# Keys in three chunks of 128 and one shared chunk of 64, instead of four chunks of 112, in an attention + MLP kernel

## The chip, the cores and the metric

The kernel runs on one core of a Trainium2 chip. The metric is the device time of one execution in microseconds (us). Timed runs of different kernels alternate with runs of the kernel before on the same chip.

## The reference

```python
# q, k, v: (8, 12, 448, 64) f32; w_in (768, 2048), w_out (2048, 768)
scores = (q @ k.transpose(0, 1, 3, 2)) / 8
attn = softmax(scores, axis=-1)
x = (attn @ v).transpose(0, 2, 1, 3).reshape(3584, 768)
h = x @ w_in
out = np.maximum(0.01 * h, h) @ w_out
```

## The kernel before

The unit of attention is a **pair** of heads (48 pairs, six to each of 8 batches). The MLP runs in eight **blocks** of 384 and 512 rows in turn; while block i runs on TensorE, the attention of batch i+1 is laid between its groups of matmuls in small bursts ("clusters").

```python
# load: three DMAs a pair, all on SP's queue; 448 rows = 112 partitions x 4 rows (1 KB runs)
for a, name, eng in zip((q, k, v), ("fq", "fk", "fv"), queues):
    t = ld_pool.tile([SC, 2, NSC, D], F32, name=name)
    eng.dma_start(out=..., in_=a[b, 2 * hp:2 * hp + 2].rearrange("h (p so) d -> p h (so d)", so=NSC))
# ... cut ...
def turn(dst, src):           # q and k of a pair by one transposing DMA (from pair 12 on)
    nc.sync.dma_start_transpose(out=dst.rearrange("p (c s) -> p c s", s=SC), in_=src)
# ... cut ...
def scores(u, c):             # one chunk of 112 keys, two heads side by side (64 rows each)
    ps = ps_s.tile([P, 2, 512], F32, name="sc")          # 3 buffers of 2 PSUM banks
    for j in range(2):
        nc.tensor.matmul(ps[:, j, :S], t[j*D:(j+1)*D, S+c*SC:S+c*SC+P], t[j*D:(j+1)*D, :S], ...)
def pv(u, j):                 # one head: 4 query chunks x 4 key chunks, 65 columns each
    ps = ps_g.tile([P, NSC, D + 1], F32, name="pv", tag="g")  # 2 banks, shared with the MLP
    for qc in range(NSC):
        for c in range(NSC):
            nc.tensor.matmul(ps[:, qc, :], e[:, at:at + P], vt[:, j, c, :], ...)
```

One cluster holds three score groups and one or two `pv`; four clusters serve three pairs. SP's queue issues, in program order, the loads, the transposes of q/k and of the attention's output x (the MLP reads x transposed, `xT`), and the stores.

The softmax here doesn't subtract the row's maximum and nothing guards it: scores larger than these inputs give would overflow.

## Time and profile before

| | before |
|---|---|
| time, median of the first 3 runs | 427.14 us (422.94 to 427.53) |
| span of the profiled run | 423.4 us |
| TensorE (PE) busy | 410.8 us (97%) |
| ScalarE (ACT) busy | 228.6 us (54%) |
| DMA issues a pair on SP | 3 loads, 2 transposes, and the stores |

The page's lines, and the chain of work in order of time, are shown in the prediction. A timeline line reads: start, duration, engine, line of the kernel, operation, output<-input, count. A name with q at the end ("SPq") is the engine's issuing of DMAs.

The table below is the yardstick: the time at which each MLP block's first matmul runs, from TensorE's timeline, as the length of each stretch. A wait in a block's first group counts in that block.

| us | start | block 0 (384) | 1 (512) | 2 (384) | 3 (512) | 4 (384) | 5 (512) | 6 (384) |
|---|---|---|---|---|---|---|---|---|
| before | 35.6 | 51.4 | 53.9 | 43.6 | 53.9 | 43.6 | 53.9 | 40.8 |

### The profile page before, as it was taken

The page shows a single profiled execution, that of the slowest core. Times are in us where ns is not written, and L with a number is a line of the kernel's source. Part 1 is how long each engine was busy: PE and PEld are TensorE (multiplying, and loading weights), DVE is VectorE, ACT ScalarE, POOL GpSimd, SP SyncE. Part 2 cuts the span into 40 slices and gives each one's busy share as a digit, 9 for nine tenths or more (in the row PEclk, how much of TensorE's full clock was granted, in tenths as well). Part 3 has the DMA queues.
Part 4 walks back from the last instruction along what each step waited for, and adds up shares of the span by engine and source line. Part 5 has one row for each costly group of instructions (what it writes and reads, how often), then busy time and mean ns, then how long its engine had stood idle before and what let it go on. Part 6 is the DMA issues. An engine that isn't in the chain of part 4 may idle for free.

```text
span 423.4 us, 9000 instructions
## 1 busy us (share of the span) xinstructions
PE 410.8 (97%) x3731; PEld 236.2 (56%) x3731; DVE 99.7 (24%) x271; ACT 228.6 (54%) x322; POOL 91.2 (22%) x168
## 2 busy tenths in 40 slices
PE   8889999999999999999999999999999999999995
PEld 3555656554556656554565656655465666654562
DVE  1542323320132212221132212321032211320021
ACT  4875772766724684467634486457652577214200
POOL 5493330530311211131131213131120200000000
PEclk9987999999999999999999999999999999999999
DMA  8999999995465947667365775768266420230022
GB/s 217 261 250 245 249 250 210 232 242 116 106 160 155 209 110 183 186 160 173 97 150 150 200 143 133 192 158 211 64 154 162 118 56 16 58 86 2 0 76 74
DMA packets 98506, 63.66 MB, mean 150 GB/s; under 512 B 55457, under 2 KB 94881, under 8 KB 98465
## 3 DMA queue, kind: packets, MB, share of 16 engines
q1 hardware_dynamic: 90928, 56.56, 54.7%
q0 software_dynamic: 7296, 6.29, 9.2%
q8 instruction: 29, 0.48, 0.5%
q10 hardware_dynamic: 240, 0.23, 0.2%
q14 instruction: 13, 0.10, 0.1%
HBM read 45.61 MB, written 11.01 MB: 134 GB/s over the span
## 4 chain that ended last, share of the span: by engine, by line
PE 92%; DMA 4%; DVE 1%; ACT 1%; SPq 0%; issue 0%; POOL 0%; ACTq 0%
PE mm L268 35%; PE mm L250 34%; PE pv L199 12%; PE sc L181 10%; DMA fk<-in_k_dram 3%; DMA fv<-in_v_dram 1%; PE tr L169 1%; DVE o L272 1%; DVE x L207 1%; ACT e L190 0%; SPq L97 0%; DVE rec L206 0%; PE tr L220 0%; DVE qkT L172 0%; POOL qkb L109 0%
## 5 line engine op out<-in xcount | busy, mean ns | idle before, releaser
L190 ACT ACTIVATE e<-sc 112x896 bf16<-112x896 f32 x192 | 164.7, 918 | 105.7 <-PE sc L181 105.4
L250 PE MATMUL mm<-xT,w_in_sb 128*128 128x384 bf16 (+1 forms) x768 | 150.6, 353 | 0.7 <-DVE x L207 0.7
L268 PE MATMUL mm<-w_out_sb,h 128*128 128x384 bf16 x896 | 150.5, 326 | 0.6 <-DVE x L207 0.3
L268 PEld LDWEIGHTS <-h 128*128 128x128 bf16 x896 | 85.8, 98 | 55.4 <-DVE x L207 0.5
L250 PEld LDWEIGHTS <-w_in_sb 128*128 128x128 bf16 x768 | 73.1, 98 | 66.6 <-DVE x L207 1.0
L254 ACT ACTIVATE h<-mm 128x384 bf16<-128x384 f32 (+1 forms) x128 | 69.7, 545 | 60.5 <-PE mm L250 60.5
L110 POOL CAST v<-fv 112x512 bf16<-112x512 f32 x48 | 29.6, 617 | 212.8 <-PE pv L199 187.3
L199 PEld LDWEIGHTS <-e 112*128 112x128 bf16 x1536 | 57.7, 99 | 30.1 <-issue 17.8
L199 PE MATMUL pv<-v,e 112*128 112x65 bf16 x1536 | 67.0, 196 | 2.6 <-ACT e L190 1.4
L272 DVE COPY o<-mm 128x384 f32<-128x384 f32 x56 | 31.2, 558 | 133.7 <-PE mm L268 133.7
L206 DVE RECIPROCAL rec<-pv 112x4 f32<-112x4 f32 x96 | 17.6, 183 | 159.2 <-PE pv L199 159.1
L181 PE MATMUL sc<-qkT 64*128 64x448 bf16 x384 | 50.2, 361 | 0.8 <-DVE qkT L172 0.4
L207 DVE TENSOR_TENSOR x<-pv,rec 112x256 bf16<-112x256 f32 x96 | 40.7, 424 | 3.3
L108 POOL CAST qkb<-fq 112x512 bf16<-112x512 f32 x47 | 28.9, 616 | 20.8 <-DMA qkT<-qkb 11.7
L109 POOL CAST qkb<-fk 112x512 bf16<-112x512 f32 x47 | 28.9, 616 | 11.3 <-DMA fk<-in_k_dram 11.2
L181 PEld LDWEIGHTS <-qkT 64*128 64x128 bf16 x384 | 13.7, 95 | 19.9 <-issue 10.4
L172 DVE COPY qkT<-tr 128x896 bf16<-128x896 bf16 x12 | 7.4, 620 | 11.7 <-PE tr L169 11.6
L169 PE MATMUL tr<-ident,qkb 112*128 112x112 bf16 x96 | 8.3, 236 | 1.4 <-POOL qkb L109 1.4
L169 PEld LDWEIGHTS <-qkb 112*128 112x128 bf16 x96 | 6.3, 110 | 3.8 <-POOL qkb L109 1.6
L135 PE MATMUL mm<-warm 128*128 128x512 bf16 x15 | 5.8, 531 | 1.2 <-DVE warm L130 1.2
L221 DVE COPY xT<-tr 128x448 bf16<-128x448 bf16 x9 | 3.5, 389 | 7.3 <-PE tr L220 7.3
L220 PE MATMUL tr<-ident,x 112*128 112x112 bf16 x36 | 3.7, 232 | 0.2
(17 smaller groups left out, 15.2 us busy)
## 6 DMA issues: line engine op xcount, KB each, us to landing
fq<-in_q_dram SPq DMA_DIRECT2D x48, 224.0 KB, 3.6
fv<-in_v_dram SPq DMA_DIRECT2D x48, 224.0 KB, 4.3
fk<-in_k_dram SPq DMA_DIRECT2D x47, 224.0 KB, 3.8
w_in_sb<-in_moe_w_in_dram POOLq DMA_DIRECT2D x4, 768.0 KB, 15.0
w_out_sb<-in_moe_w_out_dram POOLq DMA_DIRECT2D x4, 768.0 KB, 35.2
out_dram<-o SPq DMA_DIRECT2D x8, 336.0 KB, 3.0
out_dram<-o SPq DMA_DIRECT2D x8, 288.0 KB, 2.6
out_dram<-o SPq DMA_DIRECT2D x8, 240.0 KB, 3.2
```

The source lines that it names most:

```text
L108: by[0](qk_sb[u][:, 0].rearrange("p so h d -> p h so d"), fq)
L109: by[1](qk_sb[u][:, 1].rearrange("p so h d -> p h so d"), fk)
L110: by[2](v_sb[u % NV][:, :, :, :D], fv)
L169: nc.tensor.transpose(tr[:, i, ts(so, SC)], qk_sb[u][:, i, so], ident[:SC, :SC])
L181: nc.tensor.matmul(ps[:, j, :S], t[j * D:(j + 1) * D, S + c * SC:S + c * SC + P], t[j * D:(j + 1) * D, :S], start=True, stop=True,)
L190: nc.scalar.activation(e[:, :, c, :], sc_t.pop((u, c))[:SC, :, :S], AX.Exp, scale=scale)
L199: nc.tensor.matmul(ps[:, qc, :], e[:, at:at + P], vt[:, j, c, :], start=(c == 0), stop=(c == NSC - 1),)
L207: nc.vector.tensor_mul(x_t[u][:, :, j, :], ps[:SC, :, :D], rec.to_broadcast([SC, NSC, D]))
L250: nc.tensor.matmul(ps[:, :n], w_in_sb[:, kk, ts(m, P)], xT[:, kk, at:at + n], start=(kk == 0), stop=(kk == KD - 1),)
L254: nc.scalar.activation(h[:, m, :n], ps[:, :n], AX.Prelu, alpha=0.01)
L268: nc.tensor.matmul(ps[:, :NW], h[:, m, ts(c, P)], w_out_sb[:, m, ts(w, NW)], start=(m == 0), stop=(m == MD - 1),)
L272: nc.vector.tensor_copy(o[c][:, ts(w, NW)], ps[:, :NW])
```

## The change

Each head's 448 keys become three chunks of 128 and a rest of 64. The rests of both heads of a pair share one chunk: their k stand block-diagonally (128 rows of contraction), so one full-array matmul gives both heads' scores, and their v stand block-diagonally, so one product of 130 columns adds to both heads. A pair then has 3 full score groups and one half one instead of 4, 28 products instead of 32, and 3.5 exponentials' worth of columns instead of 4. The bursts become "events", two to a pair: event 0 has the first half of the last pair's products and three score groups; event 1 has the single score group and the second half.

```diff
-        for a, name, eng in zip((q, k, v), ("fq", "fk", "fv"), queues):
+        (the load of q, as before: cut)
+        for a, name, eng in ((k, "fk", queues[1]), (v, "fv", queues[2])):
+            t = ld_pool.tile([P, (2 * NKC + 1) * D], F32, name=name)
             eng.dma_start(
+                out=t[:, :2 * NKC * D].rearrange("p (h e) -> p h e", h=2),
+                in_=a[b, heads, :NKC * P].rearrange("h (p c) d -> p h (c d)", c=NKC),
             )
+            for h in range(2):
+                eng.dma_start(
+                    out=t[h * KR:(h + 1) * KR, 2 * NKC * D:], in_=a[b, 2 * hp + h, NKC * P:]
+                )
 ... (casts and zero fills cut)
-            turn(qkT[u % NQ][:, :QL], qk_sb[u].rearrange("p i so h d -> p (i so h d)"))
+            turn(qkT[u % NQ][:, :S], qk_sb[u % NC][:SC, :QC], SC)
+            turn(qkT[u % NQ][:, S:], qk_sb[u % NC][:, QC:], P)
 ...
+        if c == NKC:
+            nc.tensor.matmul(ps[:, 0, :S], t[:, keys], t[:, :S], start=True, stop=True)
+            return
 ...
+            nc.tensor.matmul(
+                ps[:, i].rearrange("p j d -> p (j d)"), e[:, at:at + P], vt[:, VL:],
+                start=True, stop=False,
+            )
 ... (first(), event() in place of cluster(): cut)
```

More of the change, by code (lines that the diff above doesn't have):

```diff
@@ L37 @@
     NW = DM // 2
+    NKC = 3
+    KR = S - NKC * P
     NU = B * HP
@@ L47 @@
     ld_pool = ctx.enter_context(tc.tile_pool(name="ld", bufs=5))
-    cast_pool = ctx.enter_context(tc.tile_pool(name="cast", bufs=4))
+    cast_pool = ctx.enter_context(tc.tile_pool(name="cast", bufs=1))
     v_pool = ctx.enter_context(tc.tile_pool(name="vones", bufs=1))
@@ L60 @@
     ps_g = ctx.enter_context(tc.tile_pool(name="ps_g", bufs=2, space=PSUM))
+    DV = D + 1
+    VL = 2 * NKC * DV
     NV = 5
-    v_sb = [v_pool.tile([SC, 2, NSC, D + 1], BF16, name=f"v{i}") for i in range(NV)]
+    v_sb = [v_pool.tile([P, VL + 2 * DV], BF16, name=f"v{i}") for i in range(NV)]
+    v_whole = [t[:, :VL].rearrange("p (h c d) -> p h c d", h=2, c=NKC) for t in v_sb]
     NE = 3
-    EL = 2 * NSC * S
-    e_sb = [exp_pool.tile([SC, EL + P - SC], BF16, name=f"e{i}") for i in range(NE)]
+    EW = 2 * NKC * S
+    EL = EW + S
+    e_sb = [exp_pool.tile([P, EL + P - SC], BF16, name=f"e{i}") for i in range(NE)]
+    NC = 4
+    QC = NSC * P
+    qk_sb = [cast_pool.tile([P, QC + (NKC + 1) * P], BF16, name=f"qkb{i}") for i in range(NC)]
     NQ = 4
-    QL = 2 * S
-    qkT = [qk_pool.tile([P, QL + P - SC], BF16, name=f"qkT{i}") for i in range(NQ)]
+    QL = S + (NKC + 1) * P
+    qkT = [qk_pool.tile([P, QL], BF16, name=f"qkT{i}") for i in range(NQ)]
     NX = 4 * S
@@ L85 @@
     raw = {}
-    qk_sb = {}
     def load(u, queues=(nc.sync,) * 3):
@@ L93, in load, with cast @@
         b, hp = divmod(u, HP)
-        raw[u] = []
-        for a, name, eng in zip((q, k, v), ("fq", "fk", "fv"), queues):
-            t = ld_pool.tile([SC, 2, NSC, D], F32, name=name)
+        heads = slice(2 * hp, 2 * hp + 2)
+        fq = ld_pool.tile([SC, 2, NSC, D], F32, name="fq")
+        queues[0].dma_start(
+            out=fq.rearrange("p h so d -> p h (so d)"),
+            in_=q[b, heads].rearrange("h (p so) d -> p h (so d)", so=NSC),
+        )
+        raw[u] = [fq]
+        for a, name, eng in ((k, "fk", queues[1]), (v, "fv", queues[2])):
+            t = ld_pool.tile([P, (2 * NKC + 1) * D], F32, name=name)
             eng.dma_start(
-                out=t.rearrange("p h so d -> p h (so d)"),
-                in_=a[b, 2 * hp:2 * hp + 2].rearrange("h (p so) d -> p h (so d)", so=NSC),
-            )
+                out=t[:, :2 * NKC * D].rearrange("p (h e) -> p h e", h=2),
+                in_=a[b, heads, :NKC * P].rearrange("h (p c) d -> p h (c d)", c=NKC),
+            )
+            for h in range(2):
+                eng.dma_start(
+                    out=t[h * KR:(h + 1) * KR, 2 * NKC * D:], in_=a[b, 2 * hp + h, NKC * P:]
+                )
             raw[u].append(t)
-    def cast(u, by=(nc.gpsimd.tensor_copy,) * 3):
+    def cast(u, by=(nc.gpsimd.tensor_copy,) * 2):
         if u >= NU:
@@ L106, in cast @@
         fq, fk, fv = raw.pop(u)
-        qk_sb[u] = cast_pool.tile([SC, 2, NSC, 2, D], BF16, name="qkb")
-        by[0](qk_sb[u][:, 0].rearrange("p so h d -> p h so d"), fq)
-        by[1](qk_sb[u][:, 1].rearrange("p so h d -> p h so d"), fk)
-        by[2](v_sb[u % NV][:, :, :, :D], fv)
+        t, vt = qk_sb[u % NC], v_sb[u % NV]
+        by[0](t[:SC, :QC].rearrange("p (so h d) -> p h so d", so=NSC, h=2), fq)
+        by[1](
+            t[:, QC:QC + NKC * P].rearrange("p (c h d) -> p h c d", c=NKC, h=2),
+            fk[:, :2 * NKC * D].rearrange("p (h c d) -> p h c d", h=2, c=NKC),
+        )
+        for h in range(2):
+            at, c0 = slice(h * KR, (h + 1) * KR), QC + NKC * P + h * D
+            by[1](t[at, c0:c0 + D], fk[at, 2 * NKC * D:])
+        nc.gpsimd.tensor_copy(
+            v_whole[u % NV][:, :, :, :D],
+            fv[:, :2 * NKC * D].rearrange("p (h c d) -> p h c d", h=2, c=NKC),
+        )
+        for h in range(2):
+            at, c0 = slice(h * KR, (h + 1) * KR), VL + h * DV
+            nc.gpsimd.tensor_copy(vt[at, c0:c0 + D], fv[at, 2 * NKC * D:])
     w_steps = []
@@ L139 @@
     make_identity(nc, ident)
-    for t in v_sb:
-        nc.gpsimd.memset(t[:, :, :, D:], 1.0)
+    for t in qk_sb:
+        nc.gpsimd.memset(t[:, QC + NKC * P:], 0.0)
+    for t, tw in zip(v_sb, v_whole):
+        nc.gpsimd.memset(tw[:, :, :, D:], 1.0)
+        nc.gpsimd.memset(t[:, VL:], 0.0)
+        for h in range(2):
+            nc.gpsimd.memset(t[h * KR:(h + 1) * KR, VL + h * DV + D:VL + (h + 1) * DV], 1.0)
     for t in e_sb:
         nc.gpsimd.memset(t[:, EL:], 0.0)
-    for t in qkT:
-        nc.gpsimd.memset(t[:, QL:], 0.0)
-    cast(0, (nc.vector.tensor_copy, nc.scalar.copy, nc.gpsimd.tensor_copy))
+    cast(0, (nc.vector.tensor_copy, nc.scalar.copy))
     load_w()
@@ L154, with turn @@
     NPE = 12
-    def turn(dst, src):
-        nc.sync.dma_start_transpose(out=dst.rearrange("p (c s) -> p c s", s=SC), in_=src)
+    def turn(dst, src, rows):
+        nc.sync.dma_start_transpose(out=dst.rearrange("p (c s) -> p c s", s=rows), in_=src)
     def dma_transposes(u):
         if NPE <= u < NU:
-            turn(qkT[u % NQ][:, :QL], qk_sb[u].rearrange("p i so h d -> p (i so h d)"))
+            turn(qkT[u % NQ][:, :S], qk_sb[u % NC][:SC, :QC], SC)
+            turn(qkT[u % NQ][:, S:], qk_sb[u % NC][:, QC:], P)
     def transposes(u):
@@ L165, in transposes @@
             return
-        tr = ps_g.tile([P, 2, S], BF16, name="tr", tag="g")
-        for i in range(2):
-            for so in range(NSC):
-                nc.tensor.transpose(
-                    tr[:, i, ts(so, SC)], qk_sb[u][:, i, so], ident[:SC, :SC]
-                )
-        nc.vector.tensor_copy(qkT[u % NQ][:, :QL], tr.rearrange("p i s -> p (i s)"))
+        tr = ps_g.tile([P, QL], BF16, name="tr", tag="g")
+        t = qk_sb[u % NC]
+        for so in range(NSC):
+            nc.tensor.transpose(tr[:, ts(so, SC)], t[:SC, ts(so, P)], ident[:SC, :SC])
+        for c in range(NKC + 1):
+            nc.tensor.transpose(
+                tr[:, S + c * P:S + (c + 1) * P], t[:, QC + c * P:QC + (c + 1) * P], ident
+            )
+        nc.vector.tensor_copy(qkT[u % NQ], tr)
     sc_t = {}
@@ L179, in scores, with expo @@
         sc_t[u, c] = ps
+        keys = slice(S + c * P, S + (c + 1) * P)
+        if c == NKC:
+            nc.tensor.matmul(ps[:, 0, :S], t[:, keys], t[:, :S], start=True, stop=True)
+            return
         for j in range(2):
+            at = slice(j * D, (j + 1) * D)
+            nc.tensor.matmul(ps[:, j, :S], t[at, keys], t[at, :S], start=True, stop=True)
+    def expo(u, c):
+        ps = sc_t.pop((u, c))
+        if c == NKC:
+            o, i = e_sb[u % NE][:, EW:EL], ps[:, 0, :S]
+        else:
+            e = e_sb[u % NE][:, :EW].rearrange("p (j c s) -> p j c s", j=2, c=NKC)
+            o, i = e[:, :, c, :], ps[:, :, :S]
+        nc.scalar.activation(o, i, AX.Exp, scale=scale)
@@ L181, in scores, with pv @@
+    def pv(u, half):
+        e, vt = e_sb[u % NE], v_sb[u % NV]
+        two = NSC // 2
+        ps = ps_g.tile([P, two, 2, DV], F32, name="pv", tag="g")
+        for i in range(two):
+            qc = half * two + i
+            at = EW + qc * SC
             nc.tensor.matmul(
-                ps[:, j, :S],
-                t[j * D:(j + 1) * D, S + c * SC:S + c * SC + P],
-                t[j * D:(j + 1) * D, :S],
-                start=True, stop=True,
-            )
-    def expo(u, c):
-        e = e_sb[u % NE][:, :EL].rearrange("p (j c s) -> p j c s", j=2, c=NSC)
-        nc.scalar.activation(e[:, :, c, :], sc_t.pop((u, c))[:SC, :, :S], AX.Exp, scale=scale)
@@ L192, in pv @@
-    def pv(u, j):
-        e, vt = e_sb[u % NE], v_sb[u % NV]
-        ps = ps_g.tile([P, NSC, D + 1], F32, name="pv", tag="g")
-        for qc in range(NSC):
-            for c in range(NSC):
-                at = (j * NSC + c) * S + qc * SC
-                nc.tensor.matmul(
-                    ps[:, qc, :], e[:, at:at + P], vt[:, j, c, :],
-                    start=(c == 0), stop=(c == NSC - 1),
-                )
-        if j == 0:
+                ps[:, i].rearrange("p j d -> p (j d)"), e[:, at:at + P], vt[:, VL:],
@@ L204, in pv @@
+                start=True, stop=False,
+            )
+            for j in range(2):
+                for c in range(NKC):
+                    at = (j * NKC + c) * S + qc * SC
+                    nc.tensor.matmul(
+                        ps[:, i, j, :], e[:, at:at + P], v_whole[u % NV][:, j, c, :],
+                        start=False, stop=(j == 1 and c == NKC - 1),
+                    )
+        if half == 0:
             x_t[u] = x_pool.tile([SC, NSC, 2, D], BF16, name="x")
-        rec = r_pool.tile([SC, NSC, 1], F32, name="rec")
@@ L206, in pv @@
-        nc.vector.reciprocal(rec, ps[:SC, :, D:])
+        rec = r_pool.tile([SC, two, 2, 1], F32, name="rec")
+        nc.vector.reciprocal(rec, ps[:SC, :, :, D:])
         nc.vector.tensor_mul(
-            x_t[u][:, :, j, :], ps[:SC, :, :D], rec.to_broadcast([SC, NSC, D])
+            x_t[u][:, ts(half, two)], ps[:SC, :, :, :D], rec.to_broadcast([SC, two, 2, D])
         )
@@ L215, in x_transposes @@
         if u >= NPE - 3:
-            turn(dst, x_t.pop(u).rearrange("p so h d -> p (so h d)"))
+            turn(dst, x_t.pop(u).rearrange("p so h d -> p (so h d)"), SC)
             return
@@ L291, in first @@
         load_w({2: 1, 3: 2, 4: 2, 5: 2}.get(u, 0))
+        scores(u, 2)
+        expo(u, 2)
         if u + 1 < HP:
             transposes(u + 1)
-        scores(u, 2)
         scores(u, 3)
-        expo(u, 2)
         expo(u, 3)
@@ L300, in first, with event @@
             pv(u - 1, 1)
-    def cluster(g):
-        t, r = divmod(g, 4)
-        u = 3 * t
-        chunks = [divmod(4 * u + 3 * r + x, NSC) for x in range(3)]
-        chunks = [(a, c) for a, c in chunks if a < NU]
-        heads = [[(u - 1, 0)], [(u - 1, 1)], [(u, 0), (u, 1)], [(u + 1, 0), (u + 1, 1)]][r]
-        heads = [(a, j) for a, j in heads if HP <= a < NU]
-        turned = {0: u - 2, 2: u - 1, 3: u}.get(r)
-        if turned is not None and HP <= turned < NPE - 3:
-            x_transposes(turned)
-        if len(heads) > 1:
-            pv(*heads.pop(0))
-        for a, c in chunks:
-            scores(a, c)
-        for a, c in chunks[:2]:
-            expo(a, c)
-        late.extend(chunks[2:])
-        for a, j in heads:
-            pv(a, j)
-            if j == 1 and a >= NPE - 3:
-                x_transposes(a)
-        if r < 3:
-            cast(u + 3 + r)
-            load(u + 5 + r)
-        transposes({3: u + 3, 0: u + 1, 1: u + 2}.get(r, NU))
-        if r > 0:
-            dma_transposes(u + 2 + r)
+    def event(g):
+        u, r = divmod(g, 2)
+        back = HP < u <= NU
+        if r == 0:
+            if HP < u - 1 < NPE - 3 + 1:
+                x_transposes(u - 2)
+            if back:
+                pv(u - 1, 0)
+            if u < NU:
+                for c in range(NKC):
+                    scores(u, c)
+                expo(u, 0)
+                expo(u, 1)
+                late.append((u, 2))
+            cast(u + 3)
+            load(u + 5)
+        else:
+            if u < NU:
+                scores(u, NKC)
+                expo(u, NKC)
+            if back:
+                pv(u - 1, 1)
+                if u - 1 >= NPE - 3:
+                    x_transposes(u - 1)
+            transposes(u + 1)
+            dma_transposes(u + 2)
     transposes(0)
@@ L340 @@
     x_transposes(u)
-    begin = [8 * (i + 1) + 3 for i in range(B)]
-    begin[0] = 8
+    begin = [2 * HP * (i + 1) + 3 for i in range(B)]
+    begin[0] = 2 * HP
     for i in range(B):
@@ L355, in catch_up @@
                 settle()
-                cluster(work[done])
+                event(work[done])
                 done += 1
```

## The prediction

> **What bounds the kernel now.** I read the page's busy table and slices first, then the groups, then the chain in order of time, and last the timelines of SP and of the first 40 us.
>
> ```profile
> PE 410.8 (97%) x3731; PEld 236.2 (56%) x3731; DVE 99.7 (24%) x271; ACT 228.6 (54%) x322; POOL 91.2 (22%) x168
> ...
> PE   8889999999999999999999999999999999999995
> ...
> DMA  8999999995465947667365775768266420230022
> ...
> PE 92%; DMA 4%; DVE 1%; ACT 1%; SPq 0%; issue 0%; POOL 0%; ACTq 0%
> ```
>
> The reader sees one full row: TensorE (PE). Nothing else is near its limit after slice 9 (some 95 us); before that the DMA row is full as well, and all of the chain's 4% of DMA lies there (two loads at 2.67 to 8.15 and 8.15 to 18.78 us). So from about 85 to 377 us only TensorE's own work counts; the first 35 us hang on loads, on the exponentials and on small waits.
>
> The chain in order of time, for the second MLP block (512 rows), gives what each piece costs on the path; columns are start, length, engine, line, count:
>
> ```profile
> 85.41 0.51 PE pv L199 x16
> 85.92 0.67 PE sc L181 x6
> 86.59 0.62 PE pv L199 x16
> 87.21 5.18 PE mm L250 x24
> ...
> 99.37 0.67 PE sc L181 x6
> 100.04 0.61 PE pv L199 x16
> 100.66 5.18 PE mm L250 x24
> ```
>
> Six score matmuls take 0.67 us, sixteen products (pv) take 0.51 us after an MLP matmul and 0.62 us after scores. A 512-column MLP matmul takes 5.18/24 = 0.216 us. Four such clusters serve three pairs of heads: 4 x 0.67 + 4 x 0.62 + 2 x 0.51 = 6.18 us, or **2.06 us a pair**. Check: the stretch from 182.90 to 236.70 us is one block of 512 rows and six pairs; its MLP is 96 x 0.216 + 128 x 0.1625 = 41.5 us, and 53.8 - 41.5 = 12.3 us = 6 x 2.05.
>
> **What the Trainium skill says.** "TensorE: Matmul & The Clock Gate", section "Back-to-back issue gap": N/2.4 + 2.5 ns for a warm matmul of N columns. This trace agrees: 215.8 ns for 512, 162.5 ns (5.20/32) for 384. For 65 columns it gives 29.6 ns; the trace has 0.51/16 = 31.9, with a start-up in it. So the products are already bound by streamed columns, not by the weight loads. "TensorEngine Tiling (Array Packing)", "Key Properties": a change of tiling mode drains TensorE. The trace agrees: scores use half the rows (64*128), two heads side by side; three such couples should stream for 3 x 189 = 567 ns and take 670, and products right after them take 0.11 us more. I call it 0.11 us per change of mode. "DMA: Bandwidth & Descriptors", "Why small descriptors are slow": a fixed cost per descriptor. The trace agrees below. Same page, "Issuing engines are not separate DMA queues": issue time is "usually small relative to the DMA itself". Here it is not: SP spends 0.45 us on a load that takes the engines 0.85.
>
> **TensorE, part by part.** Products: 32 of 65 columns (2080) become 24 of 65 and 4 of 130 (2080 again). Only four fixed costs go: 4 x 2.5 = 10 ns, say 0.50 for each half. Scores: 4 couples of 448 columns become 3 couples and one full-array matmul of 448 (about 189 ns): the same streaming time. What really goes is changes of mode: before, four clusters per three pairs, two changes each, 2.67 a pair; after, one burst of three groups a pair, 2 changes, while the fourth group runs in the products' mode. New pair: 0.67 + 0.19 + 2 x 0.50 + 0.11 = **1.97 us**, a gain of 0.09. Over 42 pairs beside the MLP: **-3.8 us**.
>
> **ScalarE.** Before 4 x 0.918 = 3.67 us a pair; after three of these and one of 448 columns, about 0.5 (the 128x384 activation takes 0.492): 3.25. ScalarE is 54% busy and not on the path after 40 us; in the first six pairs it is partly on it, worth at most 6 x 0.4 = 2.4 us. I count 1, as the loads pace that stage too. DVE keeps its work; GpSimd goes from three casts to seven a pair but is 22% busy.
>
> **Loads, the cost.** From the DMA view of 0 to 20 us:
>
> ```profile
> q1 hardware_dynamic: 3875, 3.71, 74.8%
> q0 software_dynamic: 784, 0.79, 23.2%
> q10 hardware_dynamic: 240, 0.23, 3.5%
> ```
>
> Packets, MB, share of 16 engines. q1 and q10 carry the 1 KB rows: 0.783 x 320 engine-us / 4115 = 61 ns each; q0 (weights, 2 KB read) 95 ns. A line through both: 27 ns + 34 ns per KB. So 768 B cost 53 ns and 256 B 36 ns, as estimates. Per engine and pair: now 3 tensors x 14 x 61 = 2.56 us; then 14 x 61 + 2 x (16 x 53 + 8 x 36) = 3.12 us, **22% more**. DMA is full until about 75 us, so this delays loads there: the k of pair 4, on the path at 18.8 us, by about 9 tensors x 0.28 = 2.5 us. Less 1 for the exponentials: **+1.5 us** at the start. Later pairs up to 12 slip by 6 to 12 us against the weight loads; the casts of pairs 9 and 10 are done some 10 us ahead of their transposes now, and the new order asks for them up to 9 us later. I count **+1 us**.
>
> **SP, the hidden cost.** The timeline of SP for one pair around 109 us (start, duration):
>
> ```profile
> 109.07 0.58 SPq L97 DMA_DIRECT2D fq<-in_q_dram  x1
> 109.69 0.46 SPq L97 DMA_DIRECT2D fk<-in_k_dram  x1
> 110.19 0.46 SPq L97 DMA_DIRECT2D fv<-in_v_dram  x1
> 110.77 1.28 SPq L157 DMA_TRANSPOSE qkT<-qkb  x1
> 114.83 1.19 SPq L157 DMA_TRANSPOSE xT<-x  x1
> ```
>
> An issue costs about 0.5 us and a transposing DMA 1.2 with either 4 or 8 blocks, so it goes by count. Now a pair takes 1.7 + 1.3 + 1.24 + about 0.5 (stores) = 4.7 us of SP; then seven loads (3.6), three transposes (3.7) and stores (0.5): **7.8 us**. The order view shows the seven and the two; it also shows each issue waiting for the DMA eight before it, which now covers barely more than one pair. A pair's period by TensorE is 43.1/6 = 7.2 us beside a 384-row block and 53.2/6 = 8.9 beside a 512-row one. So SP, in order, falls behind by about 0.6 us a pair, 3.5 us at the end of a 384-row block, and catches up in the next. What is late is the transpose of the last x of a batch, which the next MLP block reads as its sixth contraction step. It is issued one event (2.6 us of MLP and 1.3 of the last event) before that block starts; plus 1.0 us until the sixth step that is 4.9. DVE needs 0.8 and the transpose lands 2.5 us after issue: 1.6 us to spare. A lag of 3.5 costs about 2 us, at two such ends: **+4 us**. At the end of the first block the last two events fall together, without the 2.6 us of MLP between: 1.3 + 1.0 of cover against 3.3 and some lag, in full DMA traffic: **+3 us**.
>
> **Sum.** -3.8 + 1.5 + 1 + 4 + 3 = +5.7 us. As lags are guesses I discount them somewhat: about +3 on 427.1, **430 us**.
>
> **Rivals.** (1) TensorE alone decides, SP's lag is absorbed (loads run five pairs ahead, the q/k transposes two): 427 - 4 - 1 = 422. For it: 97% busy. Against it: SP at 7.8 of 7.2 us has no spare. (2) SP becomes the bound for good, because the eight-back wait also bites when latencies are 3 to 4 us: at 8.5 us a pair over 36 pairs (306 us against 290 now) 440 us or more. Against it: loads end six pairs before the attention does. (3) The weights and the smaller packets starve pairs 8 to 13 between 40 and 85 us, stalling TensorE by 5 to 15 us; w_out already takes 35 us to land. (4) The products gain more because 32 weight loads were what paced them: 4 x 32 ns x 48 = 6 us less. Against it: 29.6 computed and 31.9 seen leave no room.
>
> **Range and chances.** Rival 1 or 4 puts the low end at 420, rivals 2 and 3 the high end at 444. A gain over 2% (under 418.6) needs twice what the counts give: 0.06. A loss over 2% (above 435.7) needs a lag only somewhat larger than I count: 0.33. Within 2%: 0.61.
>
> **What would show it.** In the chain of the changed kernel, per pair: 3 couples of scores in 0.67, one full-array score near 0.19, 14 products near 0.50, with no 0.11 after the single score. In the SP timeline seven issues of 0.45 us a pair and three transposes of 1.2, back to back in the 384-row blocks. In the waits, TensorE at the first MLP line waiting for the xT transpose at the starts of blocks 2, 4 and 6 (some us each), and none at the others. In the DMA groups more packets and a full row up to 85 us. The prediction is wrong if the small loads issue much faster than 0.45 us (then 422), if TensorE waits for casts in mid-stage (then above 440), or if the full-array score or the 130-column products cost more than their columns.

## The result, and the profile after

The changed kernel takes **487.78 us** (486.35 to 488.74, 4 runs) against 427.33 us (median of 4 runs) for the one before: ratio 1.1451, 95% interval 1.1359 to 1.1543. A ratio here is the mean time of one kernel's runs over that of the other's of the same rounds, so it is not quite the ratio of the medians. Executions in which one die ran at a lower clock are left out of the means. The prediction (430, range 420 to 444) was wrong.

From the page of the changed kernel: busy times of the engines, then three rows of the span in 40 slices (TensorE, its granted clock, the DMA engines), then the engines' shares of the chain that ended last.

```profile
PE 426.0 (87%) x3491; PEld 245.1 (50%) x3491; DVE 100.0 (21%) x271; ACT 213.9 (44%) x324; POOL 124.7 (26%) x373
...
PE   7669989367999999965999989785999989999996
...
PEclk9797999787999999997999999998899989999999
DMA  7689997465546655456455664565645662221022
...
PE 57%; DMA 20%; SPq 14%; issue 3%; POOL 2%; ACT 2%; DVE 1%; ACTq 0%; POOLq 0%
```

TensorE's row is no longer full: 87% against 97%, with dips to 3 tenths in slice 8 and to 5 tenths in slices 19 and 28. The chain was TensorE for 92% and is now for 57%; DMA has 20% and SPq, which had 0%, has 14%. TensorE is also busy for longer, 426.0 us against 410.8, although it runs 240 matmuls fewer: the clock row falls at or just after the larger dips, and the mean granted clock is 0.951 against 0.986.

What TensorE waited for in the changed kernel (us in total, times, longest):

```profile
PE sc L227 <- DMA qkT<-qkb: 19.8, 10, 7.6
PE mm L304 <- DMA xT<-x: 19.6, 6, 5.6
```

Both are transposing DMAs of SP's queue: of q and k ahead of scores, and of x ahead of an MLP block. The 39.4 us of these 16 waits are the largest part of the 60 us lost. Where they lie shows in the yardstick:

| us | start | b0 | b1 | b2 | b3 | b4 | b5 | b6 | b7 |
|---|---|---|---|---|---|---|---|---|---|
| before | 35.6 | 51.4 | 53.9 | 43.6 | 53.9 | 43.6 | 53.9 | 40.8 | 46.7 |
| changed | 42.0 | 64.2 | 62.7 | 50.4 | 62.1 | 51.4 | 61.4 | 46.2 | 46.4 |
| difference | +6.4 | +12.8 | +8.8 | +6.8 | +8.2 | +7.8 | +7.5 | +5.4 | -0.3 |

Block 0 loses 12.8 us and each of blocks 1 to 6 loses 5 to 9; block 7, which carries no attention, loses nothing. Blocks 2 to 5 hold 24 pairs in 225.3 us: 9.39 us a pair against 8.12 before (194.96/24).

The start scatters. The kernel `both` and the four `both_...` kernels below have the same code up to block 0, and starts of 35.3, 36.1, 38.3, 38.6 and 39.7 us. So a difference of up to some 4 us in the start is not to be read.

SP's timeline for one such pair (start, duration, count at the end):

```profile
149.18 1.25 SPq L194 DMA_TRANSPOSE xT<-x  x1
150.53 2.51 SPq L194 DMA_TRANSPOSE qkT<-qkb  x2
153.10 0.57 SPq L108 DMA_DIRECT2D fq<-in_q_dram  x1
153.73 0.45 SPq L115 DMA_DIRECT2D fk<-in_k_dram  x1
154.22 1.15 SPq L120 DMA_DIRECT2D fk<-in_k_dram  x2
155.42 0.59 SPq L115 DMA_DIRECT2D fv<-in_v_dram  x1
156.05 1.75 SPq L120 DMA_DIRECT2D fv<-in_v_dram  x2
157.90 0.99 SPq L286 DMA_DIRECT2D out_dram<-o  x2
158.99 1.23 SPq L194 DMA_TRANSPOSE xT<-x  x1
```

The durations up to the next pair's first line add up to 9.26 us of a period of 9.81: SP issues without a pause but for 0.05 to 0.1 us between lines. This pair is a dear one, as it has two stores and long issues of its last two loads. Over the 24 pairs of blocks 2 to 5, summed from the trace, the issues take 8.40 us a pair, the short spaces between them (0.15 us or less) 0.67 and longer pauses 0.31. A pair costs SP more than it costs TensorE, so SP sets the pace in 384-row and 512-row blocks alike. The four loads of 64 rows (16 KB each) take 0.59 us to issue in the median of these blocks, those of 192 KB beside them 0.46 (k) and 0.59 (v): a small load is not cheaper to issue.

### The profile page after: what moved, and what is told of

It is laid out like the page before. It is cut to its first block, busy times and chain, and to the rows that moved or that the text cites. A ratio compares the mean times of both kernels' runs of the same rounds, so it can differ in the third digit from the quotient of the medians.

```text
span 486.9 us, 9127 instructions
## 1 busy us (share of the span) xinstructions
PE 426.0 (87%) x3491; PEld 245.1 (50%) x3491; DVE 100.0 (21%) x271; ACT 213.9 (44%) x324; POOL 124.7 (26%) x373
## 2 busy tenths in 40 slices
DMA packets 120396, 64.27 MB, mean 132 GB/s; under 512 B 74272, under 2 KB 116768, under 8 KB 120352
## 4 chain that ended last, share of the span: by engine, by line
PE 57%; DMA 20%; SPq 14%; issue 3%; POOL 2%; ACT 2%; DVE 1%; ACTq 0%; POOLq 0%
PE mm L304 26%; PE mm L322 21%; DMA fk<-in_k_dram 8%; SPq L120 6%; DMA fv<-in_v_dram 4%; PE pv L253 4%; PE sc L227 3%; SPq L194 3%; DMA xT<-x 3%; SPq L115 3%; DMA qkT<-qkb 3%; DMA fq<-in_q_dram 2%; SPq L286 2%; ACT e L236 1%; PE pv L246 1%
## 5 line engine op out<-in xcount | busy, mean ns | idle before, releaser
L236 ACT ACTIVATE e<-sc 128x896 bf16<-128x896 f32 x192 | 150.2, 826 | 147.7 <-PE sc L227 117.5
L304 PE MATMUL mm<-xT,w_in_sb 128*128 128x384 bf16 (+1 forms) x768 | 163.8, 369 | 20.6 <-DMA xT<-x 19.6
L138 POOL CAST v<-fv 128x384 bf16<-128x384 f32 x48 | 24.3, 506 | 163.0 <-issue 85.8
L253 PE MATMUL pv<-v,e 128*128 128x65 bf16 x1152 | 59.2, 196 | 0.0
L253 PEld LDWEIGHTS <-e 128*128 128x128 bf16 x1152 | 52.5, 99 | 11.3 <-issue 4.5
L227 PE MATMUL sc<-qkT 64*128 64x448 bf16 x288 | 38.1, 365 | 21.1 <-DMA qkT<-qkb 19.8
L246 PE MATMUL pv<-v,e 128*128 128x130 bf16 x192 | 42.9, 223 | 4.9 <-POOL v L144 3.0
L131 POOL CAST qkb<-fk 128x384 bf16<-128x384 f32 x47 | 23.8, 506 | 5.0 <-DMA fk<-in_k_dram 4.0
L144 POOL CAST v<-fv 64x64 bf16<-64x64 f32 x96 | 22.4, 233 | 8.9 <-DMA fv<-in_v_dram 6.2
L137 POOL CAST qkb<-fk 64x64 bf16<-64x64 f32 x94 | 21.8, 232 | 8.2 <-DMA fk<-in_k_dram 5.2
L246 PEld LDWEIGHTS <-e 128*128 128x128 bf16 x192 | 19.1, 100 | 9.2 <-ACT e L236 1.7
L223 PE MATMUL sc<-qkT 128*128 128x448 bf16 x48 | 17.9, 372 | 0.0
```

The costliest lines, as they stand in the source:

```text
L138: nc.gpsimd.tensor_copy(v_whole[u % NV][:, :, :, :D], fv[:, :2 * NKC * D].rearrange("p (h c d) -> p h c d", h=2, c=NKC),)
L227: nc.tensor.matmul(ps[:, j, :S], t[at, keys], t[at, :S], start=True, stop=True)
L236: nc.scalar.activation(o, i, AX.Exp, scale=scale)
L246: nc.tensor.matmul(ps[:, i].rearrange("p j d -> p (j d)"), e[:, at:at + P], vt[:, VL:], start=True, stop=False,)
L253: nc.tensor.matmul(ps[:, i, j, :], e[:, at:at + P], v_whole[u % NV][:, j, c, :], start=False, stop=(j == 1 and c == NKC - 1),)
L304: nc.tensor.matmul(ps[:, :n], w_in_sb[:, kk, ts(m, P)], xT[:, kk, at:at + n], start=(kk == 0), stop=(kk == KD - 1),)
```

## The experiments

The theories before the first run: (1) **SP's count of issues** is the bound from block 1 on; (2) the **smaller packets** of 768 and 256 B slow the loads; (3) the small loads fill the **eight places in flight** (SP has at most eight DMAs in flight in its trace, before and after), so that too few bytes are on their way; (4) the new **order of events**, with less cover ahead of an MLP block, costs the waits. The texts use these numbers. All kernels gave correct results. Times are medians; a ratio is against the kernel before, with its 95% interval.

### r_batch: the same rows, fewer loads

The 64-row rests are loaded for six pairs at once, four DMAs per six pairs in place of 24.

```diff
-            for h in range(2):          # for each pair, k and v
-                eng.dma_start(out=t[h * KR:(h + 1) * KR, 2 * NKC * D:], in_=a[b, 2 * hp + h, NKC * P:])
+                eng.dma_start(          # for n = 6 pairs (1 and 5 in the first batch)
+                    out=t[h * KR:(h + 1) * KR, :n, :], in_=src[h, NKC * P:, hp:hp + n, :])
```

> The changed kernel with the four loads of the last 64 keys made once for six pairs instead of for each pair: the same bytes and the same 256 B rows, 3.3 issues a pair fewer. Theory 1 (SP's time per issue): SP's work of 9.0 us a pair falls by 2.5 and rises by 0.4, to about 6.9; TensorE is the bound again in most blocks, 428 to 442 us. Theory 2 (the DMA engines' time for small packets): nothing changes, above 475. Theory 3 (eight loads in flight are too few bytes): gains before block 1 only, about 465.

**436.6 us**, 1.0254 (1.0197 to 1.0311). Of the 60 us 51 are gone, with 117,898 packets in place of 120,396, of the same row sizes. Blocks 2 to 5 take 43.95, 54.9, 43.96 and 54.8: 8.23 us a pair. This agrees with theory 1, and with neither theory 2 (above 475) nor theory 3 (about 465).

### one_turn: one issue less a pair

q is padded to 128 rows, so that one transposing DMA serves q and k. Everything else is as in the changed kernel.

```diff
-            turn(qkT[u % NQ][:, :S], qk_sb[u % NC][:SC, :QC], SC)
-            turn(qkT[u % NQ][:, S:], qk_sb[u % NC][:, QC:], P)
+            turn(qkT[u % NQ], qk_sb[u % NC], P)
```

> The changed kernel with q padded to 128 rows, so that q and k of a pair are turned by one DMA and not two; loads as they are. Theory 1: 1.25 us of SP a pair less (9.0 to 7.7); blocks of 512 rows back to 54 us, those of 384 rows to 47, the start unchanged: 448 to 462 us. Theories 2 and 3: within 5 us of the changed kernel's 488.

**457.5 us**, 1.0751 (1.0679 to 1.0823). Blocks 2 to 5 take 8.41 us a pair, 0.98 less than in the changed kernel, for an issue of 1.25 us taken away; start and block 0, in which only two pairs' q and k are turned by DMA, stay at +4.8 and +11.7. The total came as expected, but not its place: 54 and 47 us were expected for blocks of 512 and 384 rows, and blocks 2 to 5 took 44.0, 58.1, 44.2 and 55.6. The lag that SP gathers beside a 384-row block is paid at the start of the next, 512-row one.

### both: the two together

> Both cuts together: SP about 5.6 us a pair, as much as before. Theory 1: TensorE is the bound everywhere; with the 3.8 us that the prediction counted for its work 420 to 428, without them 427 to 432. Theory 2: above 465. Theory 4 (the new order of events stalls TensorE by itself): above 440 with SP idle.

**434.9 us**, 1.0215 (1.0154 to 1.0276): a miss, though a near one. I had expected at most 432, since SP now has room. The waits for qkT came to 0.2 us, and yet blocks 2 to 5 took 43.96 and 54.15 us, 0.38 and 0.25 more than before, not 0.55 less as the count of TensorE's work says. Two things were left; the chain in order of time shows both. First, the pieces around an MLP group late in the kernel:

```profile
315.65 0.67 PE sc L247 x6
316.33 5.31 PE mm L342 x32
321.63 0.19 PE sc L243
...
322.32 2.72 PE mm L342 x16
```

The score groups and the products cost what was predicted (0.67; 0.19 for the full-array score). But the 16 matmuls of 384 columns after the single score and its products take 2.72 us, where 2.60 (16 x 162.5 ns) is due; in the blocks of 512 columns the 18 after them take 4.04, where 3.88 is due. The second thing stands at the start of block 1:

```profile
88.29 4.02 DMA xT<-x
92.35 4.65 PE mm L324 x13
```

The chain runs over the transpose of x (4.02 us); TensorE itself waited 3.4 us of it, and the 13 matmuls behind it take 4.65 us, where 2.81 (13 x 216 ns) is due: 5.2 us in all.

For the first I formed theory 5. Event 1 is now short: 0.19 for the score and 0.50 for the second half, 0.69 us. The products and the MLP share two PSUM buffers, in which TensorE's results stand until another engine has emptied them. The MLP group after the event takes the buffer that the group before it filled, and emptying that takes 0.56 us (VectorE) or 0.60 (ScalarE, 512 columns) by itself; the event, as theory 5 has it, no longer covers this with what comes before and after it. These numbers alone do not show it; both_own below does.

### r_act: the small loads on another queue

```diff
-                eng.dma_start(
+                nc.scalar.dma_start(        # the four 64-row loads of a pair
```

> The four small loads of each pair issued from ScalarE's queue instead of SP's: counts, bytes and the eight in flight (shared by both queues) stay. Theory 1: SP falls to 6.5 us a pair, ScalarE rises by 2.5 (to some 75% busy): 430 to 450 us. Theory 2: above 475. Theory 3: the blocks recover, the start up to block 1 stays at about 113 us: 445 to 455.

**494.6 us**, 1.1624 (1.1543 to 1.1704): slower than the changed kernel, a miss for theories 1 and 3 (theory 2 had said above 475). What TensorE waited for:

```profile
PE tr L209 <- ACT qkb L131: 17.8, 1, 17.8
PE sc L227 <- ACT e L236: 13.2, 3, 7.7
PE mm L304 <- ACT h L308: 13.0, 16, 1.5
```

TensorE now waits for ScalarE. As it seems, an issue on ScalarE's queue waits there for earlier DMAs, and the work behind it in program order waits with it: ScalarE itself once waited 21.1 us for a load of v, at the start. The total says nothing on theory 1, but the places do. All the loss is in the start, 70.3 us against 42.0; blocks 0 to 6 are 23 us shorter than in the changed kernel (375.4 against 398.5), and TensorE's waits for transposing DMAs fell from 39.4 us to 4.1. So SP was relieved, as theory 1 says, and a queue of a computing engine is still no free place for issues that wait.

### b_tiny_split: SP's count alone, put on the kernel before

The kernel before, with its order, its score groups and its loads, gets four useless loads of 16 rows x 256 B a pair, and the transposing DMA of q and k is split in two.

```diff
+            if a is not q:
+                for i in range(2):
+                    d = dm_pool.tile([16, D], F32, name="dm")
+                    eng.dma_start(out=d, in_=a[b, 2 * hp + i, :16])
...
-            turn(qkT[u % NQ][:, :QL], qk_sb[u]...)
+            for i in range(2):
+                turn(qkT[u % NQ][:, i * S:(i + 1) * S], qk_sb[u][:, i]...)
```

> The kernel BEFORE with four useless loads a pair on SP's queue (16 rows of 256 B each, 16 KB a pair) and its q/k transpose split into two DMAs of the same bytes: the number of SP's issues of the changed kernel without its chunks, packets, casts, score groups or order. Theory 1: SP at about 9 us a pair, 465 to 495 us. Theory 2 (packets and bytes): below 433, as the engines get 2% more to do. Theory 4 (order of events): below 433.

**459.5 us**, 1.0803 (1.074 to 1.0866): a miss in size. It lies 5.5 us under the range of theory 1 and far above that of the others. SP's timeline shows why it is less than expected (a count of 2 covers two issues):

```profile
203.46 0.44 SPq L98 DMA_DIRECT2D fk<-in_k_dram  x1
203.95 0.92 SPq L106 DMA_DIRECT2D dm<-in_k_dram  x2
```

A load of 16 rows takes 0.46 us to issue, one of 64 rows took 0.58; over blocks 2 to 5 SP's issues take 7.86 us a pair, not 8.40. Blocks 1 to 6 took 60.8, 43.6, 59.9, 43.6, 61.3 and 40.8: SP's lag, gathered in a 384-row block, comes out whole in the 512-row block after it (waits for xT of 3.7, 4.2 and 4.5 us at the starts of blocks 1, 3 and 5), and over blocks 2 to 5 a pair takes 8.68 us. Not one matmul of this kernel differs from the kernel before. Start and block 0 lost 7.6 and 6.4 us too.

### b_packets: smaller packets alone

The kernel before, its k and v fetched in rows of 256 B: the same number of loads, 163,017 packets in place of 98,506.

```diff
+                in_=a[b, 2*hp:2*hp + 2].rearrange("h (so p) d -> p (h so) d", so=NSC),   # k and v
```

> The kernel BEFORE with k and v read in rows of 256 B instead of 1 KB (another order of the keys, the same for both; result stays right): three issues a pair as before, four times the packets of these two loads. By 36 ns a packet the engines get 2.3 us a pair more, four times what the change adds. Theory 2: at least as slow as the changed kernel, above 480. Theory 1: blocks 2 to 6 keep their 43.6 and 53.9 us, and only the load-bound start up to block 1 grows, by 5 to 20 us: 432 to 448.

**441.8 us**, 1.0387 (1.0324 to 1.045), and the yardstick puts all of it in three places: start +10.0, block 0 +7.6, block 1 +1.5. Blocks 2 to 6 are those of before to 0.1 us. So theory 2 is false for the steady part, and true for the stage in which the DMA engines are full.

### both_room and both_room_early: theory 5, with a fault of mine

The second half's products go into the spare bank of the single score's tile, so that they take no buffer from the MLP; the second kernel also begins each block one event earlier (`+4` for `+3`), so that a piece of MLP covers the transpose of x again.

```diff
-                pv(u - 1, 1)
+                pv(u - 1, 1, room=sc_t[u, NKC])     # ps = room[:, 1, :...]
```

> Both cuts, and the second half of the products written into the free second bank of the single score's tile instead of a bank of the pool that the MLP uses. In the run with both cuts the 18 MLP matmuls after such a half take 4.04 us where 3.89 are due, and 16 take 2.72 where 2.60 are due. Theory 5 (that event is too short, 0.69 us, to cover the 0.55 to 0.60 us in which ScalarE or VectorE empties the bank the next MLP group needs): the 0.12 to 0.16 us go, once for each of 42 pairs: 5 us less, about 430. Rival (a cost of the full-array score or of the 130-column products themselves): the same 435.

> The same with every block taking up the next batch's events one event earlier, so that the last x of a batch is turned one MLP step (2.6 us) earlier. In the run with both cuts block 1 starts with 3.4 us of waiting for that transpose and some 1.8 us at a lower clock. If this wait is the order's alone: 5 us less than the run before it, about 425 and within 1% of the kernel before. If the loads of the first 85 us are what is late, the wait only moves: about 430.

**464.8 us**, 1.0933 (1.0879 to 1.0988), and **464.7 us**, 1.0938 (1.0889 to 1.0988): two misses. The chain of the first shows the fault:

```profile
290.69 0.20 PE sc L243
...
290.92 0.55 ACT e L256
...
291.51 0.22 PE sc L269
...
292.17 2.60 PE mm L345 x16
```

The tile being shared, the products wait for the exponential that reads the score beside them, 0.8 us at every event 1. But the last line is what was asked: with the buffer out of the way the 16 matmuls take 2.60 us. The earlier begin took away the wait for xT at block 1, unseen under the fault.

### both_own and both_own_early: theory 5, clean

The second half's products get a tile of their own from the scores' pool; then the earlier begin on top.

```diff
+        if own:
+            bank = ps_s.tile([P, 2, 512], F32, name="sc")
+            ps = bank[:, 0, :two * 2 * DV].rearrange("p (i j d) -> p i j d", i=two, j=2)
```

> The test of theory 5 again, as the run meant for it made the products wait for the exponential of the tile that they shared: now the second half of the products gets a tile of its own from the pool of the score groups. Theory 5: the MLP group after it takes 2.60 us for 16 and 3.89 for 18 (2.72 and 4.04 with both cuts alone), 42 times 0.12 to 0.16 less in the 512-row stretches and VectorE-emptied ones: 3 to 6 us less than both cuts alone, 429 to 432. Rival: no change, 435, if the score groups now wait for that tile instead.

> The same with each batch's events taken up one event earlier. If block 1's start stalls (3.4 us and a lowered clock) only because its last x is turned in the block's last step: 4 to 6 us less again, 424 to 427, within 1% of the kernel before. If the stall moves to another wait for late loads: no change.

**429.8 us**, 1.0118 (1.0087 to 1.0149), and **428.0 us**, 1.0090 (1.0062 to 1.0119). From the chain of the first:

```profile
291.69 0.19 PE sc L243
...
292.38 3.88 PE mm L328 x18
```

The 18 matmuls take 3.88 us again, and the blocks 53.3 and 43.0: 0.58 less than before in each, where 6 pairs x 0.09 = 0.54 were counted. The earlier begin shortens block 1 from 58.9 to 53.3, as expected; the total is a miss all the same, 1.8 us less and not 4 to 6, as start and block 0 were 3.1 us longer in its profiled run. What is left against the kernel before lies ahead of block 1: 92.5 us (39.7 + 52.8) against 87.0. How much of that is the scatter of the start is not shown; `both`, whose start has the same code, had 87.7.

### mixed: the old form first, the new one after

Pairs 0 to 11 keep the loads and clusters of before; the rest have the new form with all four mends (batched rests, one transposing DMA, a tile of their own for the second half, the earlier begin).

> The first two batches (pairs 0 to 11) in the old form of four chunks of 112 with the old order, the rest in the new form with batched rests, one transpose, own tile for the second half and events one earlier. Theory: blocks 1 to 5 in the new form take 53.3 and 43.0 us where the old take 53.9 and 43.6 (seen in the two runs before), and the start keeps the old form's full-size loads until pair 12: start of block 1 at 87 to 89 us (old 87, new form 92.5), total 421 to 424, 0.991 to 0.999 of the kernel before. If the loads of pairs 12 and on already meet the weights' traffic with their smaller packets: block 1 starts late by 2 us or more and nothing is won, 424 to 427.

**424.2 us** (422.3 to 425.0), 0.9973 (0.994 to 1.0006), at the upper end of what was expected: the interval holds 1, so it is not shown to be faster. Its blocks 1 to 5 are 53.3 and 43.0 in turn, and TensorE had no wait at all of 0.1 us or more listed after 80 us. The span of the profiled run is 420.5 us, 2.9 under that of before.

## Why the prediction was wrong

**The step that failed** is "SP, in order, falls behind by about 0.6 us a pair ... and catches up in the next", worth +4 us. The mechanism, SP's count of issues and the late transposes, was right; the term was mis-sized. The prediction summed SP at 7.8 us a pair: 3.6 for seven loads, 3.7 for three transposes, 0.5 for stores. Over the 24 pairs of blocks 2 to 5 the trace has 4.03 for the loads (0.58 each, where "seven issues of 0.45 us" were looked for), 3.79 for the transposes and 0.59 for the stores, 8.40 in all, and 0.67 in the short spaces between issues, which the sum left out: 9.07 us. So blocks 2 to 5, with two of the ends that +4 was counted for, lost 30.3 us. Between 7.8 and 9.1 lies the threshold: 8.1 us is what TensorE needs over a pair of blocks. Under it SP catches up in the 512-row block; over it nothing is caught up. one_turn happens to be the case that the prediction had in mind: its SP takes 7.8 us a pair (7.23 and spaces of 0.58), and blocks 2 to 5 lose 5.6 us against the run `both`, with waits for xT at the two 512-row starts, where the prediction has +4. b_tiny_split shows the cause by itself (8.68 us a pair with the matmuls of before), r_batch its removal (8.23). That the loads end some pairs ahead of the attention did not help: the transposes stand behind them in the same queue.

SP as the bound for good is rival 2, which the prediction named ("8.5 us a pair ... 440 us or more") and gave too small a chance. Its outcome came true, but not its reason, the wait for the DMA eight before: in blocks 2 to 5 of the changed kernel, counted from the issues and landings in the trace, SP never has more than six DMAs in flight, and no issue waits for the one eight before it. Such waits stand in the start and block 0 alone, 22 us in 24 waits, and the kernel before had 29 us of them there. So that rival 2 fits is in part luck.

The sign was incomplete too. The prediction, which counts blocks from one, looked for waits at the starts of blocks 2, 4 and 6 alone. They came there (blocks 1, 3 and 5 here: 5.65, 5.01 and 4.38 us), with smaller ones at the other starts (0.7 to 2.3 us), but the 19.8 us of waiting for qkT, half of all, had no term. And the discount of the sum from +5.7 to +3 had no measurement behind it.

**The waits had a second price** that no term held: a wait of 5 us costs TensorE its clock. In the changed kernel, at the start of block 1, the 13 matmuls after a wait of 5.65 us (the chain has the last 2.54 us of it as DMA):

```profile
110.57 2.54 DMA xT<-x
...
113.16 5.70 PE mm L304 x13
```

5.70 us where 2.81 is due; the granted clock in this stretch is 0.50. It was 0.64 after a wait of 2.29 us (block 6) and stayed at 1.00 after waits of 0.71 and 1.60 us (blocks 2 and 4).

**"+1.5 us at the start" and "+1 us" for pairs up to 12** were +19.2 us; 9.2 of the 12.8 in block 0 are two waits for qkT, of the first pairs turned by DMA. The sum counted only DMA engine time for the new packets, 22% more per pair. That the weights' queue (q0) competes for the same engines stands in rival 3 ("stalling TensorE by 5 to 15 us"), whose outcome came true but which had no place in the sum; that at most eight of SP's DMAs are in flight was named, without a cost. DMA queues from 40 to 60 us (packets, MB, share of 16 engines), before:

```profile
q0 software_dynamic: 2805, 2.26, 70.5%
q1 hardware_dynamic: 2803, 2.68, 49.6%
```

and after:

```profile
q0 software_dynamic: 3027, 2.65, 82.9%
q1 hardware_dynamic: 2705, 1.63, 36.9%
```

Before, both queues get the same number of packets. After, q1 gets nearly as many, but they hold 603 bytes in the mean and not 956, so it moves 39% fewer bytes; q0 moves more. The Trainium skill, "DMA: Bandwidth & Descriptors", section "Queues, rings and completion order", says that an engine takes turns between the queues that have work, packet by packet. The trace of before agrees (2805 and 2803), and so does r_batch's (2955 and 2951); b_packets does not (3465 on q0, 3926 on q1), and whether the profile's packet is the page's is not shown. The small loads also take about half of the eight places: eight loads in flight were 8 x 224 KB before, and hold about one pair (672 KB) and a little after. b_packets shows that packet size alone can cost 17.6 us in this stage, at 3 times the packets of a pair (2016 for 672, by the shapes) where the change makes 1.5 times (992). b_tiny_split shows that the count of loads, with 64 small packets a pair more, can cost 14.1. r_batch, with the change's rows but few loads, lost only 1.4 in start and block 0 together. So the count weighs more, as it seems; but r_batch also fetches the small rows at other times, the start scatters by some 4 us, and how the 19.2 us divide stays open.

**TensorE's -3.8 us** was counted rightly, and was not to be seen. Each piece came as predicted: 0.67 for three couples, 0.19 for the single score, 0.50 for a half, no 0.11 after the single score. What was left out is that a shorter event uncovers the emptying of a PSUM buffer, 0.12 to 0.16 us at one MLP group per pair, which takes the 0.09 back and more. both against both_own shows it: 54.15 and 43.96 become 53.3 and 43.0, by a buffer alone.

**"+3 us" at the end of the first block** was the right mechanism, at 8.5 us in the changed kernel (5.65 of wait, 2.9 of clock) and, with SP relieved, 5.2 us in the run `both` (3.4 and 1.8); the earlier begin removed it.

**What no run could settle** is why the issue of a load takes from 0.42 to 0.65 us with no order by size (medians of each load's line), and whether mixed beats the kernel before.

## What to carry to other kernels

Treat the queue that issues DMAs as an engine: multiply every issue of a period by its duration in the trace, count the gaps and the stores, and compare with the bound's period; where the two are nearly equal, a few issues more decide (8.68 us a pair in b_tiny_split against 8.12 before). Splitting a load was paid here by the piece, not by the byte (0.59 us to issue 16 KB, 0.46 or 0.59 for 192 KB), and where the DMA engines were full, the queue with small rows lost bandwidth to the one with large rows (1.63 MB for 2.68 in 20 us). When work on the bound is shortened, ask what that work was covering: here 0.09 us a pair was saved and 0.12 to 0.16 uncovered.

## What the Trainium skill lacked or had wrong

- "DMA: Bandwidth & Descriptors", section "Issuing engines are not separate DMA queues", calls issue time "usually small relative to the DMA itself" and gives no figure in that section. (A table elsewhere on the page has cycles for an earlier generation, in a part on trn3.) Here loads of 192 KB took 0.46 and 0.59 us to issue, those of 16 KB 0.59, a transposing DMA 1.22, all in the median, and the sum of them was the bound: 9.1 us a pair with the spaces between them, where TensorE needs 8.1.
- "TensorE: Matmul & The Clock Gate", section "Back-to-back issue gap", gives about 131 ns as the sustained spacing at N = 512 and about 81 at N = 128 with a weight load for each matmul. Here each matmul has its weight load and the spacing was 215.8 ns at 512 columns, some 60 at 130 and 31.9 at 65; the formula that the section calls isolated (215.8, 56.7 and 29.6) fits all three.
- "TensorEngine Tiling (Array Packing)", section "Key Properties", names the drain at a change of tiling mode without a duration. Here it was 0.10 to 0.11 us a change.
